# The order of 2,836 steps: an SSM convolution beside linear attention, on one core

## The chip, the core and the metric

The kernel runs on one core of a Trainium2 chip. The core has a tensor engine (PE), a vector engine (DVE), a scalar engine (ACT), GpSimd (POOL) and a queue that issues DMAs (SP). The metric is the time of one execution on the device, in microseconds (us); lower is better.

## What is computed

Two halves are computed and joined along the last axis. The first is a state-space convolution over 2,048 positions and 576 channels, the second an attention with a learned feature map over 32 heads of 18.

```python
# A: K from 128 complex exponentials per channel, then a long convolution by FFT
P = jnp.exp((A * dt[:, None])[:, :, None] * pos[None, None, :])
K = 2.0 * jnp.einsum("dn,dnl->dl", C, P).real
y = jnp.fft.irfft(Uf * Kf[None, :, :], L2)[:, :, :L]      # Uf, Kf: rfft of u and K
a = y + u * D_skip
# B: two softmaxes per head as features, linear attention, an output projection
pq = jnp.einsum("bhsd,hdf->bhsf", q, w_phi)               # pk likewise
phi_q = jnp.concatenate([_softmax(pq, axis=-1), _softmax(-pq, axis=-1)], axis=-1)
kv = jnp.einsum("bhsf,bhsd->bhfd", phi_k, v)
o = jnp.einsum("bhqf,bhfd->bhqd", phi_q, kv) / den
b = o @ wo
return jnp.concatenate([a, b], axis=-1)
```

## The kernel before

All of the work is written first as a list of 2,836 operations, and only then issued. `Plan.op` (line 195) records one operation: its engine, what it reads and writes, and a function that issues its instructions. `body` (line 428) makes the list. `Plan.run` (line 229) goes through the text `ORDER` (line 279 on), takes the operations in that order, gives each buffer the slot that `ORDER` names, and issues them. Each engine works through its own instructions strictly in that order and waits with semaphores for the others.

An entry of `ORDER` reads as follows: the number of the operation; `*` when the second of two possible engines takes it; `!` when ACT loads a function table ahead of it; `+28` for 28 warm-up matmuls; and, after slashes, the slots of the buffers that it is the first to use. Many copies out of PSUM can go to ACT or DVE (`copy`, line 450, whose instructions stand under L453), many elementwise steps between SBUF tiles to DVE or POOL (`tt`, line 460, under L463). There are eight PSUM banks (`ps`), and nearly every PE step needs one to four of them.

The stages, in the names of the code:

- `fold` (497): `wphi` is folded into the key and query weights, in five pieces of heads. Each piece loads a block of the weight (tiles `e`, `ub`, `kvb`) and multiplies it with `wphi` (tile `fT`). PE's output goes into `wh` and `wl`, the high and low parts of the weight. `whole` (524) splits the other weights the same way.
- `key_tile` and `query_tile` (621, 686): 16 tiles of 128 positions each. A projection of 14 matmuls per half or third (`gemm`, 557), two softmaxes (`softmax`, 579: maxima and minima L586 and L587, exponential on ACT L594, pair sums on POOL L597, sums on DVE L598), and products over the heads. The query tiles turn their features by PE transposes (L701), multiply them with the key-value block `kvb`, and project the result.
- `u_first`, `group`, `k_first`, `product`, `last` (757, 926, 975, 1024, 1110): the convolution, by short Fourier steps on PE and elementwise products on DVE. `group` makes the exponentials: PE spreads magnitudes into three banks (L939's loop), ACT takes exponentials (L946), DVE multiplies them with sines and cosines (L950, L467, L954, L956) into `cs` and `E`, and PE sums them in 32 short matmuls, which the profile shows as 64.

Every matrix product is issued from line 448, every DVE or ACT copy from 453.

Of the kernel before, what the change touches and what calls it, by code (L numbers as in the profile page):

```python
# [284 lines left out]
1504 387 1332 1290/5/3/1/7/6 55/4 1293 1333 1292 43/7 1503 275/1 1508 1501 1465 1330/8 388*/2 1291 1328 1466 56/5 274
1502 48 1331/9 1507 1467 1339/1 276/10 131/3 59/0 1509/8 1340 44 389* 1334 1335 45 1510 1336 272/6 234/9 390 73 58 61
391/10 1337 60/9 1197/4 185/11 1294 132/7 62 277 392/2 278 212/12 1468 239/13 240/5 393/3 241* 213/11 63 394 1256/0
1341 214* 1237/14 280*/2 1469 381/3 398 1338 64*/4 215* 65* 1343 57/7 1505/1 104/15 1238/12 74 1344 1519 396 399*
1207/16 270/0 66! 1345 1208/10 242* 273/5 1342 290 369/17 1512 1346 1470 133* 1239 217/7 221/4 134 1199/14 1347/18 395
67/3 289 220 222/3 1426/1 1472 1672 1473 243/1 1511 1471 1531/0 1387/1 279 245/5 250/3 262*/13 1513 1514 1427 281 282  # L290
251 246/3 68/1 252/8 1385 1428 1348 69/0 218/6 263 1386 1198 70* 1533 1200/5/7/4/1/12 1515 1516 71* 75* 76 283/4 1201*
1202* 1506 223 1517 1388 261 284/0 1474/3/0/5/13/9 1476 1255 1429 1518 1520 1204 1477 1430 224 226/1 244/7 1481 1480
1203 1475 247 248 158/8 1431 159/2 1296 347/3 348/5 235 1674 1295 1479 135/2 378/3 216/4 138/4 155/4 1534 225 349*
1487/6/5/1/6/0 1488 249 1679 285/4 227 1490 1521/6 160* 350* 207/14 1522 153 400 1432 1209 286* 1489 228 1523 54/5
219/4 253*/0 254 236 255 1524 1478 1495 287 1492 1482 137/7 1491 428/18 154 429/1 1493 1494 1525 256/16 1206 257/0
1526 229/6 1350 136/4 140/3 1240/1/6/0/3/11 230/1 1527 1241 1496/5/7/4 1528 430* 1483/1 1244 231/2 1433 1529 1217/1
1242 1484 1219*/6 1530 232 1243 1257/3 1205 139 1535/0 143 141/9 142 145/1 455/12 258/5 1536 1434 1485 237* 144 353/3
370 1166 1177/16 161 352/0 1486 1245 146* 355/1 233 356 1497 1437/1/7/4/13/12 431 1537 1498 359 351/6 358 1435 1436
1246 357/0 360 1440! 1499 354/6 1439 1444 1450/5/3/0/6/5 361/2 1538 1442 238 371 362 1453 1456 1218* 1455 1539 1540
1451 1443 1452 1458 1454 147 1438 435/6 434/4 148/1 401/8 402/3 452/9 363 1541 1441 1457 291 439/2 1210/1/5/6/0/11  # L300
1459/3 1213 1445 1212 440 1446/7 451* 441/5 1675 1211 1460 1680 259 432/7 1220/1/4/5/6/6 149/0 364/10 1317/18 1681/1
450 1214 1223 1676 1215 164/0 264 1224 365/4 1544 1221 150/1 1532 366/3 433/6 260 1683 367* 1682 372* 368* 1259/10
1685 403* 1545 1258 163/1 404* 1684 151* 156 456/12 1187/6 1216 169/3 1389/1 1390 1222 1226 152 186/1 437 1447 1225
1461 1448 436 1449 1542 170 1543 167 265 1462 438 442/0 373 1686 1687 166 408/3 168/0 181/13 443 171 1391 457*
1546/0/1/6/6/8 1547! 425* 1392 1548 1559/7/4/5/11/13 1393 1561 1351 1560 1550 1567 1563 1566 1562 172/0 157 173 77/8
1565 406/3 1549 1394 1352 1353 180 405/8 407/0 105/9 1554 410/0 444 445/4 165/4 1552 1551 1564 174 458 461/5 175/17
1395 1553 1396 413 446/3 447/2 106 1673 1677/0 182 412 424 187* 107* 1688 1689 188* 293/3 448* 1555/4 99/4 414/3
1568/1 1397 1400/0/6/7/6/8 1846 1556 1557 1403 1558 409 1401 467/3 411 466 1402 449 176/1 1690 1407 177/4 1405 459/9
1569 294/11 1570 1572/0 1406 415/5 192/4 1404 1573 1574 416 460/3 463 1408 417 209 162/10 190/7 464 1575 1576 292 178
1398 418/17 419/1 1399 194/5 179 1409/6 1571 478/11 453 1678 468/10 193 1577 420/2 189/11 465 1691 320/15 421*  # L310
1413/5/1/0/2/13 1307/12 1415! 1416 1692 469*/1 1178/7 1705/1 1693/17 1578 109/4 470* 1694 477 426* 1695 1696 471 1410
472/17 191/3 1414 1697 195/6 1844 1421 1417 321/8 322* 1411 1579 462/7 479 473/1 196 1698 1277/1 323 1699 1581 1419
422 1700 111/5 1580 1851 324/12 427 1418 1420 1422/1 128 474/2 112/3 1583/5/0/7/3/12 113 1585! 183 197 1412 1423* 198
108/13 1586 325/6 1701 208 1424 1425 475 480 1702 114/2 1584 1591 1781/1 110/3 476 1588 1587 1782 1582 1783
1622/5/4/1/13/1 1590 1624! 1589 199/2 329/5 1703 115 328 1784 116 117 1592/7 1593 1227/15 1625 200 330/3 326/0 1623
1785 327/6 1630 1786 201 78/12 118/2 1847 1626 1852 496/17 1628 127 1787 1629 202/0 344 1627 119 120 1594 184 203/3
1596 295* 1179 1631/1/8/9 1632 1854 1598/6/4/3/5/0 296* 297/14 343 1744/0 1595 1790 1863 1602 1853/3 1597 1601 1856
79* 332 1633 299/7 80 1634 1745 331 1788 1599 333 204/2 1600 1604/3/5/0/1/1 1606 1789 121/8 1267/16 1855 122/1 123/4
454 304/0 1791 298/5 484 1608 1746 1747 1748 305 334*/6 1318*/9 306/5 1607* 205* 1605* 316*/8 301 302 303 1704 335
1706 1792/7/1/3/7/13 1794! 1799 1800 1319* 1793 1795 1798 1797 336 300/0 317 307/6 1260/1/5/4/6/11 1264 481 124 1261  # L320
1749 1262 1796 1603/1 483 1805/6/3/0/0/10 1806 1263* 1807 83/1 1808 337/18 308 309 100 82/4 338/1 1609 1813 1750
1269*/11 1751 339/6 210 206 1812 89/0 81/15 1188*/18 504/1 1753 88 1811 211 1810 1809 90/6 1801/0 1610/1/6/3/7/7 125
1266 1857 340* 1802 1612 84/5 129* 1754 1752 341 86 85 91*/4 1611* 511/13 310/3 506/1 1279*/14 87 92 1803 1804 1858
1614* 1613 311/0 1265 312/1 313* 315 1297/10 1859 130 93 1616/3/7/0/4/12 1619 1814/6 101* 1617* 1848 1620*
1320/3/5/4/0/0 318 1618 1322* 1323* 1615 94/5 509 1324 505/7 1815* 1321 1860 507 1635/1 510 1180/4/3/5/0/10 1184 1183
# [831 lines left out]
```

## Time and profile before

| what | value |
|---|---|
| median of three runs | 514.7 us (512.82 to 516.24) |
| the profiled execution's own time | 511.89 us |
| its span, first to last instruction | 510.1 us |
| PE, matmuls busy | 485.1 us, 95% |
| PE, weight loads busy | 406.6 us, 80% |
| DVE busy | 450.0 us, 88% |
| ACT busy | 400.6 us, 79% |
| POOL busy | 337.0 us, 66% |
| DMA, 16 engines | 71.3% by the main queue, mean 226 GB/s |
| mean granted TensorE clock | 0.993 |

The profile is one execution. A row of its timeline has a start and a duration in us, the engine, the line, the instruction and what it writes and reads; a number in brackets at the end is the time that the engine stood idle before, and what released it. "issue" there means that nothing the profile shows was waited for. A row of the groups ends with busy time, mean nanoseconds of one instruction, and idle time before them. Busy time of PE counts matmuls with modelled ends.

### The profile page before, as it was taken

What the parts mean: (1) busy time and instruction counts of PE and PEld (TensorE: products, weight loads), DVE (VectorE), ACT (ScalarE), POOL (GpSimd) and SP (SyncE); (2) the same over time, 40 slices, a digit from 0 to 9 for tenths busy, and PEclk for the clock granted to TensorE, in tenths of its full rate; (3) what the DMA queues carried; (4) which work ended last, traced back from release to release, by engine and by line L of the source; (5) the groups of instructions that cost most, each with busy time, mean ns of one, the idle gap of its engine ahead of it and who ended that gap; (6) DMA issues with size and microseconds to landing.
All of it is one profiled execution on the core that took longest, in us unless ns stands there. A gap on an engine that the chain in (4) does not pass through costs nothing.

```text
span 510.1 us, 20535 instructions
## 1 busy us (share of the span) xinstructions
PE 485.1 (95%) x8544; PEld 406.6 (80%) x8544; DVE 450.0 (88%) x999; ACT 400.6 (79%) x704; POOL 337.0 (66%) x405
## 2 busy tenths in 40 slices
PE   5999999999999989899999999998999999999997
PEld 5999798899988878688886767775788886677976
DVE  3899999999999998999898999998999688889584
ACT  5589889899999989999999888999897535545321
POOL 1653599679878897996895379887465326476510
PEclk9799999999999999999999999999999999999999
DMA  7976974615507476771999386649696998998797
GB/s 204 351 255 189 306 219 171 190 39 197 186 27 234 143 231 192 196 255 34 302 272 352 100 267 212 215 142 298 202 324 176 330 272 245 294 370 254 269 324 213
DMA packets 80800, 115.45 MB, mean 226 GB/s; under 512 B 12612, under 2 KB 58564, under 8 KB 80708
## 3 DMA queue, kind: packets, MB, share of 16 engines
q1 hardware_dynamic: 80708, 114.14, 71.3%
q8 instruction: 67, 1.10, 0.9%
q14 instruction: 25, 0.20, 0.1%
HBM read 65.11 MB, written 49.01 MB: 224 GB/s over the span
## 4 chain that ended last, share of the span: by engine, by line
PE 57%; DVE 17%; ACT 15%; issue 4%; DMA 4%; SPq 1%; POOL 1%; DVEq 0%; ACTq 0%
PE ps L448 53%; PE ps L701 3%; ACT ps L946 2%; ACT cs L914 2%; ACT cs L922 2%; DMA e<-in_wkT_dram 2%; ACT cs L921 2%; DVE cs L950 1%; DMA x<-xd 1%; ACT e L594 1%; DVE x L463 1%; PE ps L731 1%; DVE small L463 1%; ACT zi L453 1%; DVE e L467 1%
## 5 line engine op out<-in xcount | busy, mean ns | idle before, releaser
L448 PE MATMUL ps<-wh,x 128*128 128x288 f32 (+2 forms) x1008 | 242.5, 321 | 2.2 <-DVE ks L467 1.0
L448 PEld LDWEIGHTS ps<-wh,x 128*128 128x128 f32 x1008 | 173.7, 189 | 14.8 <-issue 3.7
L448 PE MATMUL ps<-wl,x 128*128 128x288 f32 (+2 forms) x560 | 175.3, 314 | 0.9 <-issue 0.9
L448 PEld LDWEIGHTS ps<-wl,x 128*128 128x128 f32 x560 | 105.7, 189 | 1.3 <-issue 1.2
L904 POOL TENSOR_TENSOR cs<-cs,pi 128x64 int32<-128x64 int32 (+4 forms) x90 | 90.1, 1001 | 5.0
L463 POOL TENSOR_TENSOR E<-v,cs 128x512 f32<-128x512 f32 x34 | 43.2, 1287 | 25.7 <-ACT v L946 25.7
L597 POOL TENSOR_TENSOR o<-e 128x576 f32<-128x576 f32 x32 | 43.2, 1351 | 21.5 <-ACT e L594 12.7
L946 ACT ACTIVATE ps<-ps 128x512 f32<-128x512 f32 x90 | 50.0, 589 | 6.4 <-PE ps L448 5.9
L467 DVE TENSOR_TENSOR ac<-us,ps 128x576 f32<-128x576 f32 x64 | 44.7, 745 | 6.0 <-PE ps L448 5.8
L950 DVE TENSOR_TENSOR cs<-ps,cs 128x1024 f32<-128x1024 f32 x36 | 43.6, 1216 | 2.7 <-ACT ps L946 2.5
L594 ACT ACTIVATE e<-e 128x1152 f32<-128x1152 f32 x32 | 37.3, 1171 | 9.1 <-POOL e L463 9.0
L448 PEld LDWEIGHTS ps<-E,cs 128*32 128x32 f32 x2304 | 34.0, 110 | 8.8 <-issue 3.5
L448 PE MATMUL ps<-E,cs 128*32 128x64 f32 x2304 | 39.0, 220 | 1.7 <-DVE E L956 1.3
L922 ACT ACTIVATE cs<-cs,hp 128x1024 f32<-128x1024 f32 x36 | 40.3, 1146 | 0.0
L463 POOL TENSOR_TENSOR e<-e,small 128x576 f32<-128x576 f32 x26 | 32.2, 1239 | 11.7 <-DVE small L463 11.0
L453 ACT ACTIVATE zi<-ps 128x288 f32<-128x288 f32 x91 | 33.1, 410 | 8.6 <-PE ps L448 6.6
L921 ACT ACTIVATE cs<-cs 128x1024 f32<-128x1024 int32 x36 | 37.5, 1057 | 0.2
L463 POOL TENSOR_TENSOR e<-small,e 128x576 f32<-128x576 f32 x26 | 30.4, 1170 | 10.1 <-DVE small L463 2.4
L463 POOL TENSOR_TENSOR ac<-ac 128x288 f32<-128x288 f32 x31 | 24.3, 810 | 16.0 <-DVE ac L467 14.2
L914 ACT ACTIVATE cs<-cs 128x2048 f32<-128x2048 int32 x18 | 34.6, 1924 | 0.1
L886 POOL TENSOR_TENSOR pi<-pi 128x192 int32<-128x192 int32 (+1 forms) x42 | 21.1, 513 | 17.5 <-DVE pi L882 10.1
L586 DVE TENSOR_REDUCE small<-ps 128x16 f32<-128x288 f32 (+2 forms) x64 | 28.3, 444 | 4.9 <-PE ps L448 4.8
(144 smaller groups left out, 1005.3 us busy)
## 6 DMA issues: line engine op xcount, KB each, us to landing
dram<-zi SPq DMA_DIRECT2D x32, 288.0 KB
xd<-x SPq DMA_DIRECT2D x16, 576.0 KB
dram<-zi SPq DMA_DIRECT2D x16, 576.0 KB
x<-xd SPq DMA_DIRECT2D x16, 576.0 KB
kb<-dram SPq DMA_DIRECT2D x32, 288.0 KB
ub<-dram SPq DMA_DIRECT2D x32, 288.0 KB
dram<-zo SPq DMA_DIRECT2D x32, 288.0 KB
zi<-dram SPq DMA_DIRECT2D x16, 576.0 KB
```

What stands on the lines that cost most here:

```text
L448: pe.matmul(o, l, r, start=start, stop=stop, skip_group_check=skip)
L453: op(("act", "dve"), (c_act(n), c_dve(n)), lambda e: act.activation(dst(), src(), AF.Copy) if e == "act" else dve.tensor_copy(dst(), src() ...
L463: op(eng, [c_dve(n[0]) if e == "dve" else c_pool(n[1]) for e in eng], lambda e: (dve if e == "dve" else pool).tensor_tensor(dst(), a(), b( ...
L467: op(eng, c_dve(n) if eng == "dve" else c_pool(n), lambda: e.tensor_tensor(dst(), a(), b(), op=alu), r=r, w=w, with_=with_, lock=eng == "p ...
L594: op("act", c_act(1152) + 40, lambda: act.activation(e.t, e.t, AF.Exp), r=[e], w=[e], table="exp")
L597: op("pool", c_pool(517), lambda: pool.tensor_tensor(pair.t, e.t[:, :, :, 0:9], e.t[:, :, :, 9:18], op=ALU.add), r=[e], w=[pair], lock=True)
L904: op("pool", c_add(4 * n * W), lambda n=n, j=j: pool.tensor_tensor(x()[:, :, :, n:2 * n], x()[:, :, :, 0:n], pi.t[:, j:j + 2, gs].bitcast( ...
L914: op(("act", "dve"), (c_act(n) + 45, c_dve(n)), lambda e: act.activation(cs.t[:, 0], x(), AF.Abs) if e == "act" else dve.scalar_tensor_ten ...
L921: op("act", c_act(64 * W) + 150, lambda at=at: act.activation(at(1), at(1).bitcast(I32), AF.Sin, scale=TURN), r=[cs], w=[sine], with_=[cs] ...
L922: op("act", c_act(64 * W) + 225, lambda at=at: act.activation(at(0), at(0), AF.Sin, scale=-TURN, bias=hp.t), r=[cs, hp, sine], w=[both], w ...
L946: op("act", c_act(512) + 12, lambda x=x, y=y: act.activation(y.t, x.t, AF.Exp), r=[x], w=[y], table="exp")
L950: op("dve", c_dve(64 * W), lambda: dve.tensor_tensor(F(), both(M.t), F(), op=ALU.mult), r=[M, ready], w=[long], with_=[cs])
```

## The change

Only the text `ORDER` is replaced. The operations, their dependences, the numbers of slots and all functions stay as they are. The new text was found by a search that began at the old one, with a model of the chip corrected for late results, late instructions and extra waits.

```diff
 ORDER = """
-0/0 3 2 1 423/0 33 1356 1357 1362 4/1 35+28/0 34/1 49/2 1361 1363/2 1364 1366 1365 1367 1368 482 1373 5/0 342/2 1369
+0/0 1 2 234/0 1349 4/1 288/2 1354 1358 1357 1362 1356 1361 1363/3 5/0 7+28/0 1364 1365 1366 1367 1368 1369 1370 6/1
...
```

PE takes its 414 steps in nearly the same order as before: a step moves by less than one place on average and by nine at most. DVE's, ACT's, POOL's and SP's steps move by five to eleven places on average, and almost all slots are other ones, PSUM banks included. 74 copies out of PSUM go from ACT to DVE and 55 the other way; 27 elementwise steps go from DVE to POOL and 19 the other way. So DVE has 1,010 steps rather than 999, ACT 627 rather than 646, POOL 409 rather than 401. ACT loads its function tables 43 times in both. PE's stream holds 196 separate wait instructions rather than 189, ACT's 200 rather than 193, DVE's 207 rather than 219.

Three places, as the instructions stand.

The first is SP's queue at the very start. `e`, `ub` and `kvb` are the five blocks of the key weight, `fT` is `wphi`, `zo` a tile of x; `cre`, `cim`, `dt`, `th` are small parameters of the convolution. Before:

```order
L504 DMA kvb<-in_wkT_dram 72x640
L841 DMA cre<-in_cre_dram 128x96
L841 DMA cim<-in_cim_dram 128x96
L500 DMA fT<-in_wphi_dram 128x630
L504 DMA e<-in_wkT_dram 126x640
L839 DMA dt<-in_ldt_dram 128x96
L841 DMA th<-in_aim_dram 128x96
L504 DMA ub<-in_wkT_dram 126x640
L491 DMA zo<-in_xT_dram 128x640
L504 DMA e<-in_wkT_dram 126x640 x2
```

In the changed kernel the same queue begins so:

```order
L500 DMA fT<-in_wphi_dram 128x630
L839 DMA dt<-in_ldt_dram 128x96
L841 DMA cim<-in_cim_dram 128x96
L841 DMA cre<-in_cre_dram 128x96
L504 DMA e<-in_wkT_dram 126x640
L841 DMA th<-in_aim_dram 128x96
L504 DMA ub<-in_wkT_dram 126x640
L504 DMA e<-in_wkT_dram 126x640
L491 DMA zo<-in_xT_dram 128x640
L504 DMA kvb<-in_wkT_dram 72x640
L504 DMA e<-in_wkT_dram 126x640
```

The block in `kvb` moves from the front to the tenth place, the x tile behind the second `e`; the last `e` is the eleventh load in both. PE's fold follows: before, `kvb`, `e`, `ub`, `e`, `e`; now `e`, `ub`, `e`, with `kvb` between the pieces of that `e`, and the last `e`.

The second is DVE at the sixth pair of groups, just before the short matmuls that start at 212 us in the profile of before. `E<-ps,cs` are the products that those matmuls read, `small<-o` is the softmax sum of a query tile. Before:

```order
L467 TENSOR_TENSOR e<-ps,small 128x16x18
L950 TENSOR_TENSOR cs<-ps,cs 128x2x16x32
L467 TENSOR_TENSOR E<-ps,cs 128x16x32 x2
L954 TENSOR_TENSOR E<-ps,cs 128x16x32
L598 TENSOR_REDUCE small<-o 128x64
L956 SCALAR_TENSOR_TENSOR E<-ps,cs 128x16x32
L600 RECIPROCAL small<-small 128x32
```

In the changed kernel, at the same place of DVE's stream:

```order
L467 TENSOR_TENSOR E<-ps,cs 128x16x32
L950 TENSOR_TENSOR cs<-ps,cs 128x2x16x32
L467 TENSOR_TENSOR E<-ps,cs 128x16x32
L954 TENSOR_TENSOR E<-ps,cs 128x16x32
L956 SCALAR_TENSOR_TENSOR E<-ps,cs 128x16x32
L598 TENSOR_REDUCE small<-o 128x64
L600 RECIPROCAL small<-small 128x32
```

The softmax sum moves behind the last product, and one of the E products ahead of the cs product.

The third is PE at another group, at 377 us in the profile of before. `ps<-E,cs` are the group's 32 short matmuls, `ps<-kvb,fT` end a query tile's products, `wh` and `wl` with a numbered x begin or end a projection, and `ident,o` are transposes of a query tile. Before:

```order
L448 MATMUL ps<-kvb,fT 64x95 x2
L448 MATMUL ps<-kvb,fT 64x76 x2
L448 MATMUL ps<-E,cs 32x64 x32
L448 MATMUL ps<-wh,x_6823 128x288
L448 MATMUL ps<-wl,x_6823 128x288
```

In the changed kernel:

```order
L448 MATMUL ps<-wh,x_6636 128x288 x2
L448 MATMUL ps<-wl,x_6636 128x288
L448 MATMUL ps<-E,cs 32x64 x32
L731 MATMUL ps<-ident,o 128x128 x4
L732 MATMUL ps<-ident,o 128x128
```

The projection of 14 matmuls that followed the group now stands ahead of it.

More of the change, by code (lines that the diff above doesn't have):

```diff
@@ L285 @@
[L285 to L324, printed above, removed]
@@ new lines @@
+1285 1035/1 1836* 1833* 1286 2162 1036/0 1834 1037/0 1889 1032/5 1033/2 1838/6/3/2/7/0 1034 1189* 1038/5/1 857 1835
+1887 1840* 1933* 1936/0/4/11 706/0 1839* 707 1039/9 1841* 1837 1842* 1940/2/6/3/5/3 1040 1937* 858/2 855/7 1943!/0
+1041 1938 2019 2020 1942 1843 1042 1228* 1941 1939 708 1947 1944 1230/0/1/3/4/6 1233 1232 1234 859 860 1946* 1948
+1945* 1231 1236 861 1043/5 1045/0 2164 709/3 2166 710/2 1310/0/4/1/2/0 1312 1313 862/3 863 1949/6 1953/1
+1890/4/5/7/8/12 1314* 711 1311 712 1235 1954 1950 1316 1190/0/2/1/3/3 1951 1952 713* 1891 1892 1044/6 1893/6 1192
@@ new lines @@
+2327 2333 2725/5/1/13 2726 2727 670/0 2760/4/7/17 2761 1062 2728 2762 1063* 2623/1/6/3/2/1/15 671/0 1064 672 2763
+765/7/0 2737 766/3 767 673 2758 2730 2627* 2729 674* 2624 777/5 2764 782/0 972/4 976/3 781 2628/0 783/4 2629/5 2625
+977 679/2/2 680 971/7 973 2765 776/5 974 979*/5 2603/8 2602/16 978/10 677/4/13 2626 975 768 778 779 769 784/3 2522/10
+675/7/17 2630/3/2/6/1/2/13 780 678 2631 676 2767/0/4/0 2768 681/7 2635 2632 2773/11 814/12 785 786 2769
+2597/4/6/3/5/5/17 2601 2599 787/1 980 2598 2636 2637 2638 2633 2634 2770 2757 2521/7 682/0 2600 684/2 685/1
@@ new lines @@
+2604/1/5/0/6/8/0 2680/15 683/2 686 2681/13 2675/4/7/3/2/11/8 2678 2772 2513/16 2606 2610 1065/5/18 2771 2676* 2576/4
+788/1 1066 1067/6/12 2609 687/4/3 688/7 2605 2607 689 1068 2677 2608 2679* 690 770/5 772/5 2515/1 691
+2639/4/7/6/1/17/2 2640 2682/2/0/5/3/5/1 1069/4/9 789 2611 2612 2642* 692/6 1070 2641* 2569/0 2643* 2683 2684 2685 2688
+2687 2644/1 2570/13 2613/0/2/1/4/11/15 2616* 2614* 1071/7 2645 1074/5 2707/6 981 2615 694*/18 1075/0 1072/2
+2516/0/1/2/3/8/9 2518 790 791 2519 2618 1073/17 1076 794/6/12 2617* 2568/1 792/5/14 795 2523/4/1/7/2/0/8 2689 2517*
@@ L425 @@
+2827 2749 2750 1105 847 2781/7/3/13 2782* 1008 1113/2 2809/4/6/17 2810* 1114/3 813 2751 2811 2812 1115/16 2816/1/5/1
+2813 2830/6/3/7 2831* 2832 2833 2835 2817 2834 2783 2784 1110/5 1111/3 2786 2814 2785 2828 1112 2795/3/2/5 2788/6/4/11
+2789 2802/7/0/8 2790 2791 2796 2793 2803* 2818 2819 2804 2820 1116/4/5 2792 849/2 1117/2 1118 1119 2805 1120 2806
+848/1 2797 2821 2798 2800 2807 851*/13 2799 850 852 1122/5 1124/6 1121/1 1123* 1125
 """.split()
```

229 lines of the change are left out of this document (125 added, 104 removed).

## Prediction

> **What bounds the kernel now.** I read the page first (busy times, the chain that ended last), then the busy time of every engine in stretches of 50 us, because shares over the whole span mix the stages.
>
> ```profile
> span 510.1 us, 20535 instructions
> PE 485.1 (95%) x8544; PEld 406.6 (80%) x8544; DVE 450.0 (88%) x999; ACT 400.6 (79%) x704; POOL 337.0 (66%) x405
> PE 57%; DVE 17%; ACT 15%; issue 4%; DMA 4%; SPq 1%; POOL 1%; DVEq 0%; ACTq 0%
> ...
> 50.00:100.00 50.00, 47.68 (x860) 42.90 (x859) 48.73 (x106) 43.48 (x75) 38.01 (x49) 1.00 0.70 217
> 100.00:150.00 50.00, 50.00 (x801) 47.37 (x803) 47.88 (x102) 46.89 (x69) 42.38 (x52) 1.00 0.35 121
> 150.00:200.00 50.00, 47.14 (x1142) 39.31 (x1128) 46.80 (x106) 46.88 (x81) 43.10 (x46) 1.00 0.66 209
> 200.00:250.00 50.00, 47.02 (x758) 40.53 (x759) 47.32 (x115) 48.76 (x83) 41.50 (x53) 1.00 0.59 173
> 250.00:300.00 50.00, 47.45 (x1021) 37.17 (x1009) 46.08 (x104) 44.41 (x87) 32.60 (x35) 1.00 0.80 248
> 300.00:350.00 50.00, 47.73 (x1123) 35.70 (x1106) 46.33 (x102) 47.23 (x78) 43.29 (x50) 1.00 0.70 219
> 350.00:400.00 50.00, 47.72 (x988) 38.84 (x992) 45.36 (x101) 40.51 (x62) 27.95 (x26) 1.00 0.78 249
> 400.00:450.00 50.00, 49.46 (x869) 37.73 (x861) 39.91 (x90) 24.83 (x60) 21.72 (x27) 1.00 0.94 285
> ```
>
> The columns are PE, PE's weight loads, DVE, ACT and POOL, then TensorE's granted clock and the DMA engines. The tensor engine is busy 95% and carries 57% of the chain, so it bounds the kernel. But up to 350 us DVE and ACT are busy 44 to 49 of every 50 us as well: they give the banks free and make the operands that PE waits for. From 400 us on only PE is full. PE stands idle 510.1 - 485.1 = 25.0 us. Of these 15.8 us lie between 50 and 450 us (400 less the sum of the eight PE numbers, 384.2). The rest is mostly the start and the last store. An order that runs the same matrix work can win from these 25 us, and from waits hidden in PE's busy time, since matmul ends are modelled; little else.
>
> **The change, part by part.** The operations and PE's work are the same, and PE's own order moves by a few places. What changes is the start, who stands before whom on DVE and ACT, the banks, and which of two engines takes a copy or an elementwise step.
>
> *The start.* These rows give the sizes of the first loads, PE's first real work, and the clock.
>
> ```profile
> e<-in_wkT_dram SPq DMA_DIRECT2D x3, 315.0 KB
> fT<-in_wphi_dram SPq DMA_DIRECT2D x2, 315.0 KB
> ub<-in_wkT_dram SPq DMA_DIRECT2D x1, 315.0 KB
> kvb<-in_wkT_dram SPq DMA_DIRECT2D x1, 180.0 KB
> zo<-in_xT_dram SPq DMA_DIRECT2D x16, 320.0 KB
> cre<-in_cre_dram SPq DMA_DIRECT2D x6, 48.0 KB
> ...
> 6.55 1.32 PE L448 MATMUL ps<-fT,e 126*128 126x126 f32 x10
> 9.79 1.38 PE L448 MATMUL ps<-fT,ub 126*128 126x126 f32 x10 [1.92 <-DMA ub<-in_wkT_dram]
> 12.67 4.63 PE L448 MATMUL ps<-fT,e 126*128 126x126 f32 x20 [1.50 <-DMA e<-in_wkT_dram]
> 16.96 0.66 PE L448 MATMUL ps<-wh,x 128*128 128x378 f32 x1
> ...
> 8.00:9.00 1.00, 0.00 (x0) 0.00 (x0) 0.26 (x1) 0.98 (x2) 0.00 (x0) 1.00 0.93 291
> 11.00:12.00 1.00, 0.17 (x2) 0.00 (x0) 0.57 (x2) 0.63 (x1) 0.00 (x0) 0.78 1.04 224
> 16.00:18.00 2.00, 2.00 (x10) 2.00 (x9) 1.05 (x3) 1.09 (x3) 0.61 (x1) 0.50 1.11 398
> ```
>
> PE waits twice for a load of wkT, 1.92 and 1.50 us. Before the `ub` load stand 180 + 315 + 315 KB and four loads of 48 KB; with itself 1317 KB, and PE starts at 9.79. Before the second `e` come 320 KB more; with itself 1952 KB, and PE starts at 12.67. So the queue delivers (1952 - 1317) / (12.67 - 9.79) = 220 KB/us. In the new order the 180 KB load stands behind both and the 320 KB load behind the second: `ub` is in after 1137 KB, 0.8 us earlier (9.0), the second `e` after 1452 KB, 2.3 us earlier (10.4). The last `e` closes the same 2267 KB in both, at 12.67 + 315/220 = 14.1. Ten matmuls take 1.32 us at full clock, so the fold may end at 15.4, at half clock at 16.7; before, the first projection starts at 16.96. That is a gain of 0.3 to 1.6 us; I take 1.0. Other ends: if the 180 KB load, now ahead of the last fold pieces, comes a microsecond late, 1.0 is lost; if the clock did not fall at all, the 5.7 us of PE work between 12.67 and 18.4 would shrink by half of that, 2.9 more.
>
> The clock rows show 1.00 until PE has idled at 8 us and 0.50 at 16 to 18. [...]
>
> *Results that come late.* The second place is the waves' group whose matmuls start at 212.18.
>
> ```profile
> 212.18 1.10 PE L448 MATMUL ps<-E,cs 128*32 128x64 f32 x64 [1.30 <-DVE E L956]
> ...
> 210.15 0.68 DVE L954 TENSOR_TENSOR E<-ps,cs 128x512 f32<-128x512 f32 x1
> 210.77 0.75 DVE L598 TENSOR_REDUCE small<-o 128x64 f32<-128x576 f32 x1
> 211.44 0.68 DVE L956 SCALAR_TENSOR_TENSOR E<-ps,cs 128x512 f32<-128x512 f32 x1
> ```
>
> PE waits 1.30 us for the last E. On DVE a softmax sum (L598) stands ahead of it. In the new order it stands behind: E starts at 210.77 instead of 211.44, and 0.67 us of the 1.30 are gone. What is late next is the softmax sum, some 0.6 us later than before; PE's next step but one needs it, behind a POOL step. Of the 15.8 us of idle time, 5.7 are of another kind (below), so 10.1 are waits for results. This place gives half of its wait back. Other places get more lead, and others less, so the ends are 5.2 worse (the added DVE work, below) and 5.0 better (half everywhere). I take a quarter, 2.5 us, as nearer to the gain because the work on PE's path was moved forward where I looked and nothing there was moved back.
>
> *Code that comes late.* Some idle rows name no releaser. I found six; the first, the longest and the last:
>
> ```profile
> q8 instruction: 67, 1.10, 0.9%
> 186.99 0.44 PE L448 MATMUL ps<-e,v 128*19 128x36 f32 x27 [0.98 <-issue]
> 350.67 0.77 PE L701 MATMUL ps<-ident,e 128*128 128x128 f32 x5 [2.12 <-issue]
> 378.43 0.53 PE L448 MATMUL ps<-E,cs 128*32 128x64 f32 x19 [0.32 <-issue]
> ```
>
> PE's 2 x 8544 instructions come in 67 pieces, about 255 each. All six idle rows start at the same place of such a piece, counted through PE's stream, and the first and the longest follow many short matmuls. So PE ran out of code. The six last 0.32 to 2.12, in all 5.7 us. Short matmuls placed together use a piece up fastest. At 378 the new order puts a projection of 14 long matmuls ahead of the group's short ones: that row goes, 0.3 us. At 350 only the transposes trade places, and around 187 the stretch stays as dense. I take -0.3; the ends are 2.4 better (350 goes too) and 2.1 worse (one more like it).
>
> *Work that changes engine.* On DVE there are 22 more copies out of PSUM and 3 fewer of the `fT` kind, and from DVE to POOL go, net, seven splits of x and five small sums, while three `kb` steps and one of 576 columns come back.
>
> ```profile
> L453 DVE COPY zi<-ps 128x288 f32<-128x288 f32 x37 | 15.8, 447 | 3.5 <-PE ps L448 3.5
> L453 DVE COPY fT<-ps 128x512 f32<-128x512 f32 (+1 forms) x15 | 7.4, 498 | 5.6 <-PE ps L701 5.6
> L463 DVE TENSOR_TENSOR x<-zo,x 128x512 fp32r<-128x512 f32 (+1 forms) x24 | 13.3, 553 | 1.0 <-ACT x L543 0.8
> L463 DVE TENSOR_TENSOR small<-small 128x32 f32<-128x32 f32 x22 | 7.5, 343 | 0.3
> L463 DVE TENSOR_TENSOR kb<-ub 128x288 f32<-128x288 f32 x12 | 7.3, 607 | 0.0
> L463 DVE TENSOR_TENSOR e<-e,small 128x576 f32<-128x576 f32 x6 | 4.9, 819 | 0.0
> L453 ACT ACTIVATE zi<-ps 128x288 f32<-128x288 f32 x91 | 33.1, 410 | 8.6 <-PE ps L448 6.6
> ```
>
> The copies: 22 x 0.447 - 3 x 0.498 = 8.3 us more on DVE. The rest: 7 x 0.553 + 5 x 0.343 - 3 x 0.607 - 0.819 = 2.9 less. Net 5.4 us more, about 5.2 as one of the copies is only of 128 columns. ACT is relieved of 19 x 0.410 = 7.8 us. DVE has 60.1 us idle (510.1 - 450.0), which hides it: I put 0 into the sum, and the 5.2 into the rival below.
>
> DVE's `kb` step with two operands in SBUF takes 607 ns, the copy of the same size out of PSUM 447. [...]
>
> **Sum.** 511.9 (the profiled execution, its span and 1.8 us around it) - 1.0 - 2.5 - 0.3 = 508.1. The median shown, 514.7, is 2.8 above the profiled execution, so the median of the changed kernel comes to **510.9 us**, 0.7% below. Its own range is 506.5 to 515.
>
> **Rivals.** *The waits go further (faster).* Half of the result waits go (5.0), the start takes 1.6, the code waits at 350 and 378 both go (2.4): 511.9 - 9.0 + 2.8 = 505.7, with 501 as its end. For it: waits of this kind cost PE more than its idle rows show. Against it: PE's order hardly moves, and where 44 to 49 of 50 us are used on three engines, each step moved ahead puts another back.
>
> *DVE becomes the late engine (slower).* Between 150 and 350 us DVE is busy 186.5 of 200 us. Between 150 and 400 us 14 copies more, net, come to DVE, and each gives a bank free that a later matmul writes, while the steps that left for POOL were on nobody's path. If each copy holds PE up for its 0.447 us, that is 6.3 us; with nothing won elsewhere, 511.9 + 6.3 + 2.8 = 521.0. It decides from 12 of the 14 on (5.2 us, 1% of 514.7). Against it: the same copies leave ACT, which is as full.
>
> *The trades cancel* (no gain, 512 to 517): the order shows that steps did move, but PE's floor is the same; this lies within my forecast's case.
>
> **How the numbers follow.** Within 1% is about what a measurement of this kernel can tell from no change (its three runs spread over 512.8 to 516.2). Forecast and cancelling trades together, within 1%: 0.44. Further gain, faster by over 1% (below 509.6): 0.40. DVE late, slower (above 519.8): 0.16. The range 501 to 520 leaves out the best end of the first rival (0.05) and most of the second (0.15).
>
> **What would show it.** PE's fold row with `ub` at about 9.0 and the second `e` at about 10.4, the first projection before 16.7. The E row of that group without L598 ahead of it and PE's wait there about 0.6. No issue row inside the group's matmuls that now follow the projection near 378, but one still near 187. DVE busy about 455, ACT about 392, PE's idle time 21 rather than 25. Wrong would be: PE's waits for DVE between 150 and 400 us grown by microseconds, or new issue rows of over a microsecond.

## The result, and the profile after

The changed kernel takes 510.75 us, median of 22 runs (507.23 to 514.91), against 515.15 for the kernel before in the same job (22 runs, 509.91 to 519.78). The ratio is 0.9919 with a 95% interval of 0.9897 to 0.994: 0.8% faster, 4.2 us. The profiled execution took 507.23 us, against 511.89. Here and below a ratio leaves out executions more than 1.5% above the fastest one of their kernel, a median does not, and the profiled executions of the runs with two places, shift and copies were such long ones.

These are the span, the busy times and the chain of waits on the page of the changed kernel, and below them three stretches of the table by windows, with its sum over 50 to 450 us.

```profile
span 505.4 us, 20522 instructions
PE 482.6 (95%) x8544; PEld 404.6 (80%) x8544; DVE 454.6 (90%) x1010; ACT 394.9 (78%) x684; POOL 340.0 (67%) x413
PE 69%; DVE 15%; issue 4%; DMA 4%; POOL 3%; ACT 2%; SPq 1%; DVEq 0%; POOLq 0%; ACTq 0%
```

```profile
50.00:100.00 50.00, 49.16 (x827) 44.54 (x813) 48.97 (x102) 42.65 (x74) 40.08 (x55) 1.00 0.68 211
100.00:150.00 50.00, 50.00 (x897) 47.35 (x896) 49.40 (x103) 49.01 (x69) 43.59 (x54) 1.00 0.30 106
...
400.00:450.00 50.00, 48.20 (x855) 35.81 (x857) 43.33 (x97) 19.91 (x49) 26.18 (x33) 1.00 0.94 287
sum 400.00, PE 386.13 PEld 321.24 DVE 373.73 ACT 335.52 POOL 300.28; mean PE 48.27 PEld 40.15 DVE 46.72 ACT 41.94 POOL 37.53
```

PE now carries 69% of the chain instead of 57%. It stands idle 505.4 - 482.6 = 22.8 us (before 25.0), and 400 - 386.13 = 13.9 us of it lie between 50 and 450 us (before 15.8). Between 50 and 150 us, where it stood idle for 2.3 us, it stands idle for 0.8. Between 400 and 450 us it stood idle for 0.5, and now for 1.8: something was gained early, and something lost late.

The start, in PE's timeline of the changed kernel, and the clock in two windows there:

```profile
6.45 1.35 PE L448 MATMUL ps<-fT,e 126*128 126x126 f32 x10 [1.90 <-DMA e<-in_wkT_dram]
8.19 2.50 PE L448 MATMUL ps<-fT,ub 126*128 126x126 f32 x10 [0.38 <-DMA ub<-in_wkT_dram]
10.48 1.34 PE L448 MATMUL ps<-fT,e 126*128 126x126 f32 x8
...
13.12 1.41 PE L448 MATMUL ps<-fT,e 126*128 126x126 f32 x10
14.35 0.44 PE L448 MATMUL ps<-wh,x 128*128 128x378 f32 x1
```

```profile
8.00:10.00 2.00, 1.81 (x8) 1.81 (x9) 1.08 (x6) 1.33 (x6) 0.00 (x0) 0.50 0.99 269
...
14.00:16.00 2.00, 2.00 (x14) 1.99 (x13) 2.00 (x7) 1.65 (x3) 1.84 (x4) 1.00 1.03 385
```

`ub` is there at 8.19 (forecast 9.0), the second `e` by 10.48 (forecast 10.4), and the last `e` makes nothing wait at 13.12, so it was in before the 14.1 that the prediction gave it. The clock is at 0.50 in the window from 8 us and at 1.00 from 14 to 16, where it was at 0.50 before. The first projection begins at 14.35, 2.6 us earlier.

The second place, the short matmuls of the sixth pair of groups, in the timeline of the changed kernel:

```profile
204.40 0.68 DVE L956 SCALAR_TENSOR_TENSOR E<-ps,cs 128x512 f32<-128x512 f32 x1
...
205.00 0.74 DVE L598 TENSOR_REDUCE small<-o 128x64 f32<-128x576 f32 x1
...
205.20 1.10 PE L448 MATMUL ps<-E,cs 128*32 128x64 f32 x64
...
207.76 1.20 PE L701 MATMUL ps<-ident,e 128*128 128x128 f32 x9 [1.46 <-POOL e L463]
```

L956 now has the softmax sum (L598) behind it, and the wait of 1.30 at the short matmuls is gone. The next step on PE, the transposes of `e`, waits 1.46 us for POOL. In the kernel before the row of these transposes reads:

```profile
214.10 1.20 PE L701 MATMUL ps<-ident,e 128*128 128x128 f32 x9 [0.83 <-POOL e L463]
```

So 0.63 us of the 1.30 are back one step later.

These are all idle rows of PE in the changed kernel, from 16 us on, that name no releaser:

```profile
189.19 0.78 PE L448 MATMUL ps<-fT,e 72*128 72x72 f32 x5 [1.88 <-issue]
268.00 0.35 PE L448 MATMUL ps<-kvb,fT 128*64 128x76 f32 x3 [0.23 <-issue]
336.79 1.10 PE L448 MATMUL ps<-E,cs 128*32 128x64 f32 x63 [0.40 <-issue]
352.98 0.38 PE L448 MATMUL ps<-sel,mg 32*128 32x256 f32 x2 [0.74 <-issue]
364.58 0.74 PE L448 MATMUL ps<-ac,ff 32*32 32x288 f32 x21 [0.21 <-issue]
419.37 0.69 PE L448 MATMUL ps<-ub,ff 64*32 64x288 f32 x7 [0.81 <-issue]
458.98 0.67 PE L448 MATMUL ps<-ac,ff 32*32 32x288 f32 x3 [1.45 <-issue]
```

They add up to 5.72 us, against 5.67 of the six before. Counted through PE's stream of matmuls, weight loads and waits, all six of before stand 194 places behind a multiple of 256, and these seven 193 or 194. The row inside the group near 378 is gone, the one near 187 has grown from 0.98 to 1.88, and behind 400 us there are two where there was none.

What went away are waits for DVE in the first 170 us. The rows of the kernel before, and then those of the changed kernel in the same part of the work:

```profile
52.34 0.75 PE L448 MATMUL ps<-kb,w 32*64 32x288 f32 x16 [0.29 <-DVE small L463]
53.88 0.75 PE L448 MATMUL ps<-e,v 128*19 128x36 f32 x64 [0.80 <-DVE v L463]
...
99.64 0.45 PE L448 MATMUL ps<-wh,x 128*128 128x396 f32 x1 [1.01 <-DVE ks L467]
...
160.22 0.57 PE L448 MATMUL ps<-sel,mg 32*128 32x256 f32 x6 [0.44 <-DVE v L453]
```

```profile
51.06 0.57 PE L448 MATMUL ps<-sel,mg 32*128 32x256 f32 x5 [0.51 <-DMA mg<-gd]
...
85.19 0.86 PE L448 MATMUL ps<-kb,w 32*64 32x288 f32 x16 [0.26 <-DVE e L467]
```

2.54 us of waits became 0.77.

### The profile page after: what moved, and what is told of

It reads as the page before. It is cut to its first block, busy times and chain, and to the rows that moved or that the text cites. A ratio compares the mean times of both kernels' runs of the same rounds, so it can differ in the third digit from the quotient of the medians.

```text
span 505.4 us, 20522 instructions
## 1 busy us (share of the span) xinstructions
PE 482.6 (95%) x8544; PEld 404.6 (80%) x8544; DVE 454.6 (90%) x1010; ACT 394.9 (78%) x684; POOL 340.0 (67%) x413
## 4 chain that ended last, share of the span: by engine, by line
PE 69%; DVE 15%; issue 4%; DMA 4%; POOL 3%; ACT 2%; SPq 1%; DVEq 0%; POOLq 0%; ACTq 0%
PE ps L448 65%; PE ps L701 3%; DVE cs L950 2%; DVE E L467 2%; POOL cs L904 2%; PE ps L731 1%; DVE E L956 1%; DMA kb<-dram 1%; DMA gd<-cs 1%; DVE x L463 1%; DVE E L954 1%; DVE ac L467 1%; DMA ub<-in_wkT_dram 1%; DMA mg<-gd 1%; DVE e L467 1%
## 5 line engine op out<-in xcount | busy, mean ns | idle before, releaser
L463 POOL TENSOR_TENSOR e<-small,e 128x576 f32<-128x576 f32 x24 | 28.2, 1174 | 10.7 <-DVE e L467 9.8
L453 ACT ACTIVATE zi<-ps 128x288 f32<-128x288 f32 x80 | 28.9, 413 | 5.3 <-PE ps L448 5.0
```

The lines of the kernel that those rows point to most:

```text
L453: op(("act", "dve"), (c_act(n), c_dve(n)), lambda e: act.activation(dst(), src(), AF.Copy) if e == "act" else dve.tensor_copy(dst(), src() ...
L463: op(eng, [c_dve(n[0]) if e == "dve" else c_pool(n[1]) for e in eng], lambda e: (dve if e == "dve" else pool).tensor_tensor(dst(), a(), b( ...
```

## The experiments

The theory after this comparison was that the start gives the larger part of the gain, since PE is 2.6 us ahead there of 4.2 in all, that the engine choices cost nothing, and that late code gives nothing. The rivals: the start is worth the 1.0 us of the prediction and the rest lies in later waits; the copies on DVE cost time that something else wins back; the gain lies in where the pieces of code happen to begin. Every run is compared with the kernel before on the same chip, with 10 or 12 executions of each (6 where it is far slower) against 27 to 29. The kernel before had medians of 513.4 to 514.2 us in these jobs.

### The loads and the fold of the new start alone

In the text of the order this is the beginning:

```diff
-0/0 3 2 1 423/0 33 1356 1357 1362 4/1 35+28/0 34/1 49/2 1361 1363/2
+0/0 3 2 1 423/0 4/1 1354 1357 1362 1356 49/2 1361 1363/2
...
+5/0 7+28/1 6/0 126/5 1369 1355 1358 1370 19/4 21/3 1359/0 1360
```

> The kernel before, with only the start of the changed kernel: the order of the first eleven loads, of the ten fold steps on PE with their banks, of the copies and low parts that empty them, and the one clearing of a tile on POOL that has to wait for the old place of the 180 KB block. Everything from the first projection on is as before. If the start is the larger part of the gain, the first projection begins at 14.3 to 15.0 us rather than 16.96, its first matmuls run at full clock, and the time falls by 2.6 to 3.3 us (ratio 0.9935 to 0.995). If the start is worth the 1.0 us of the prediction, because what PE wins there it waits for again in the first projections (for x tiles and copies), the ratio is 0.997 to 0.999. If the whole gain came from later waits, the ratio is 1.000.

Measured: 515.61 us, ratio 1.0044 (1.0011 to 1.0078): slower, which none of the three expected. PE's timeline:

```profile
14.20 1.98 PE L448 MATMUL ps<-fT,kvb 72*128 72x72 f32 x8 [2.36 <-DVE wl L516]
...
18.91 0.66 PE L448 MATMUL ps<-wh,x 128*128 128x378 f32 x1
```

In the new order of the fold a bank comes round sooner. The low part that has to empty it stood on DVE behind the split of an x tile, PE waited 2.36 us, and the first projection began at 18.91, 2 us later than before. The loads are no gain without the steps on DVE and POOL that go with them.

### The whole start

As above, and DVE's, ACT's and POOL's order up to the first projection too, with the x split (376, 377) on POOL and one `kb` step (1249) on DVE.

```diff
-19/4 21/5 126/5 374/6 12/1 375/0 376* 1377 377*
+374/6 33 10 1377 1378 1379 26/2 375/0 376 1380 377 8 49/2 22 11
```

> The kernel before with the whole start of the changed kernel: loads, fold and banks as in the run with the new start, and also the order of DVE, ACT and POOL up to the first projection, with the first x split on POOL instead of DVE and one kb step on DVE instead of POOL. Behind the first projection everything is as before. In the run with the new start alone PE waited 2.36 us in the fold for a low part (wl, L516) on DVE, which stood behind the x split. If that wait was all that spoiled it, the first projection begins at 14.3 to 14.8 us and PE stays 2.6 to 3.3 us ahead to the end, since the 2 to 3 us that the earlier run had lost by 30 us were still lost at the end: ratio 0.993 to 0.996. If later steps take the lead back (loads of x and u, which this order does not move), PE is ahead by less than 1 us at 60 us and the ratio is 0.998 to 1.002.

Measured: 512.45 us, ratio 0.9987 (0.9963 to 1.0012): 0.7 us, with an interval from 1.9 better to 0.6 worse. In its timeline the first projection comes at 15.07. Then come three rows around the sixth pair of groups, and the window with the clock behind the second:

```profile
15.07 0.44 PE L448 MATMUL ps<-wh,x 128*128 128x378 f32 x1
...
209.86 1.10 PE L448 MATMUL ps<-E,cs 128*32 128x64 f32 x64 [1.30 <-DVE E L956]
211.78 2.01 PE L701 MATMUL ps<-ident,e 128*128 128x128 f32 x9 [0.82 <-POOL e L463]
...
220.23 1.58 PE L448 MATMUL ps<-kvb,fT 128*64 128x76 f32 x40 [0.37 <-ACT fT L453]
```

```profile
211.00:214.00 3.00, 2.22 (x17) 1.89 (x25) 3.00 (x6) 2.47 (x6) 3.00 (x3) 0.67 0.78 213
```

Up to 209.86 PE is 2.3 us ahead of the row at 212.18 of the kernel before. At 220.23 it is 1.2 ahead of the same row there, which reads:

```profile
221.41 1.63 PE L448 MATMUL ps<-kvb,fT 128*64 128x76 f32 x40 [0.37 <-ACT fT L453]
```

Between the two the clock fell to 0.67, right behind waits of 1.30 and 0.82 us that lie together; in the profile of before two such waits (1.30 and 0.83) left it at 1.00 over the whole stretch from 200 to 250 us. So the lead of 2.3 us was carried through 190 us of work, and 1.1 of it went in the stretch with this one fall of the clock. For the other executions no trace shows where their part went.

### The changed kernel with the old start

```diff
-0/0 2 1 234/0 1349 4/1 288/2 1354 1358 1357 1362 1356 1361 1363/3 5/0 7+28/0
+0/0 2 1 234/0 49/4 33 288/2 1356 1357 1362 1361 4/1 1363/3 5/0 35+28/2
```

> The changed kernel with the start of the kernel before put back: loads, fold, the order of ACT and DVE up to the first projection, the x split on DVE and the kb step on POOL. The rest is as changed. If the start is worth 3.3 us of the 4.4, this lies at a ratio of 0.997 to 1.000 to the kernel before and the first projection begins at about 17. If the start is worth 1.0, as predicted, the ratio is 0.993 to 0.995, and the gain lies in what follows.

Measured: 510.96 us, ratio 0.9943 (0.9916 to 0.9971). Against the 0.9919 of the changed kernel, measured in another job, the start is worth 0.0024, 1.2 us, with 1.8 either way (the half intervals added as squares), and what follows it 0.0057, 2.9 us, with 1.4 either way. The run before gave 0.7 for the start and allows 1.9 at most, so the theory falls. The prediction's 1.0, about a quarter of the gain, fits both runs, but neither of them tells it from nothing.

The 2.6 us at the first projection are one pair of executions, too. In the six profiles with the old loads and no filler it begins at 15.90 to 18.65 us, 17.3 in the mean, and in the five with the whole new start and no filler at 14.35 to 15.68, 15.1 in the mean.

### The clock held up by filler

```diff
-35+28/0
+35+37/0
-21/5
+21+17/5
-13/7
+13+13/7
```

> The kernel before with more idle matmuls on zeros at the start: 37 rather than 28 ahead of the first fold piece, 17 in the wait for the ub load, 13 in the wait for the second e load. Nothing else moves. If the clock is what the start loses, it stays at 1.00: the twenty matmuls that took 4.63 us from 12.67 on take 2.6 to 2.8, the first projection begins at 15.2 to 15.5 and its first 1.4 us run at full clock too, in all 2.0 to 2.9 us less (ratio 0.994 to 0.996). If the loads are the limit, the last e makes PE wait until 14.1 and the gain is about 0.7 to 1.5. If the clock falls for another reason than idle PE, nothing changes. The 39 matmuls more are also 78 more instructions in front of everything else in PE's stream. If the idle rows without a releaser (186.99, 196.11, 274.85, 281.47, 350.67, 378.43) are late pieces of code, they do not stay at their work: each turns up about 78 instructions earlier in the work, longer or shorter as the work there uses code up faster or slower, and the 2.12 us in front of the transposes near 350 are gone from there. If they are waits for something that the profile does not show, they stay where they are.

Measured: 516.03 us, ratio 1.0038 (1.0005 to 1.007): slower. The wait for `ub` and the end of the fold:

```profile
10.57 1.38 PE L448 MATMUL ps<-fT,ub 126*128 126x126 f32 x10 [0.84 <-DMA ub<-in_wkT_dram]
...
13.22 2.91 PE L448 MATMUL ps<-fT,e 126*128 126x126 f32 x20
```

The twenty matmuls took 2.91 us instead of 4.63, with the clock at 1.00 (the window below). But `ub` came 0.8 us later in this execution (10.57 for 9.79), then a copy (ACT, 0.58) became the limit, and the first projection came at 16.71, only 0.25 us earlier. At the wait for `v` PE was 0.9 us ahead (52.97 for 53.88), and it stayed about so up to 190 us.

All six rows without a releaser of the kernel before are gone from their work, the one ahead of the transposes near 350 too, and seven others stand elsewhere. In PE's stream they stand as before: all seven 193 or 194 places behind a multiple of 256, and four of them (near the 6,082nd, 8,642nd, 8,898th and 11,970th place) where four of the six stood. The wait keeps to its place in the stream while other work comes to stand there. That fits pieces of code (the page of the kernel before and that of the changed kernel show 67 packets of the instruction queue, about 255 of PE's matmuls and weight loads each) and not a hidden wait of the work itself.

In the end the kernel is 0.4% slower. In these two profiles the rows without a releaser do not account for it (5.96 us for 5.67). From 16 us on, PE's waits for DVE grew from 6.2 to 8.5 us and those for ACT from 1.8 to 2.9; why is open. The window of the clock:

```profile
12.00:17.00 5.00, 4.42 (x35) 3.76 (x33) 4.36 (x13) 4.25 (x12) 3.00 (x8) 1.00 1.03 347
```

### Code moved by 34 places in the changed kernel

```diff
-7+28/0
+7+45/0
```

> The changed kernel with 45 rather than 28 idle matmuls on zeros ahead of the first fold piece, where PE waits 1.9 us for a load anyway. It moves every later instruction of PE by 34 places in its stream and costs PE nothing at the start. If late code depends on where the pieces of about 256 instructions begin in the work, and the order was fitted to that, the idle rows without a releaser all move to other work and grow together, and the time is 3 to 8 us longer: ratio to the kernel before 0.998 to 1.008. If the pieces do not matter, the time stays within 1 us of the changed kernel's 510.7, ratio 0.990 to 0.994, perhaps a little less because the clock does not fall at 7.7 us.

Measured: 515.12 us, ratio 1.0 (0.9962 to 1.0039). 17 idle matmuls, put where PE waits anyway, cost 4.2 us (2.3 either way), as much as the whole gain. The first projection begins at 15.56, as in the other profiles with this start. The longest of its ten rows without a releaser:

```profile
351.41 0.83 PE L701 MATMUL ps<-ident,e 128*128 128x128 f32 x3 [3.23 <-issue]
```

The rows have moved to other work again, and one of 1.01 us, at 56 us, is in a stretch where neither kernel had any. In this profile the ten add up to 12.44 us, against 5.72; that the other executions lose as much there is not shown. So the gain of the changed kernel also hangs on the places at which its code breaks into pieces. For the order before this is not shown: under the filler its rows add up to hardly more (5.96 for 5.67).

### Two of the moves alone

```diff
-1139/6 630 1654
+630 1654 1139/6
-2254/6 ... 738/3
+738/6 ... 2254/3
```

> The kernel before with two of the moves of the changed kernel alone: on DVE the softmax sum (L598) behind the last E product ahead of the short matmuls at 212.18, and on PE the projection of 14 matmuls ahead of the group's short matmuls near 377 (with their two banks exchanged). The first: E starts at 210.8 rather than 211.44 and PE's wait of 1.30 there falls to about 0.6. If that is a gain, PE stays 0.6 us ahead at 220; if it is given back, the wait for POOL at the next transposes grows by about as much (0.9 to 1.5). The second: the idle row without a releaser inside the short matmuls (0.32) goes. Together 0.3 to 0.9 us if neither is given back (ratio 0.998 to 0.9995), 0 to 0.3 if the first is.

Measured: 513.89 us, ratio 0.9981 (0.9945 to 1.0018): no difference that can be seen. At the first place:

```profile
215.65 1.10 PE L448 MATMUL ps<-E,cs 128*32 128x64 f32 x64 [0.60 <-DVE E L956]
...
218.27 0.99 PE L701 MATMUL ps<-ident,e 128*128 128x128 f32 x7 [1.52 <-ACT wh L531]
```

The wait is 0.60 instead of 1.30, exactly as worked out, and the next wait 1.52 instead of 0.83. From the E row to the transposes the kernel before takes 214.10 - 212.18 = 1.92 us, this one 218.27 - 215.65 = 2.62. All 0.70 us are given back, and the order of the two DVE steps explains it. The transposes wait for POOL's step on `e`, that step for the reciprocal (L600), and the reciprocal stands on DVE behind the last product and the softmax sum in either order. In the kernel before:

```profile
212.04 0.34 DVE L600 RECIPROCAL small<-small 128x32 f32<-128x32 f32 x1
```

In this one:

```profile
216.29 0.35 DVE L600 RECIPROCAL small<-small 128x32 f32<-128x32 f32 x1
...
217.05 1.16 POOL L463 TENSOR_TENSOR e<-e,small 128x576 f32<-128x576 f32 x1
```

From the start of L954 to the reciprocal it is 1.89 us before (210.15 to 212.04) and 1.97 here (214.32 to 216.29), and to the transposes 3.95 in both. The profile names ACT's L531, which ended 0.07 us behind POOL's step. At the second place the row without a releaser inside the group is gone, as expected.

### Only the engine choices, in the old order

175 entries gain or lose their `*`; two of them:

```diff
-1254 ... 1201* 1202*
+1254* ... 1201 1202
```

> The kernel before in its own order and banks, with only the choice of engine taken from the changed kernel: 74 copies from ACT to DVE, 55 the other way, 27 elementwise steps from DVE to POOL, 19 the other way. By the prediction the 5 us more of DVE work are hidden: DVE busy about 455, ACT about 393, the ratio 0.998 to 1.003. By the rival in which DVE becomes late, each copy more holds PE up: PE's waits for DVE grow between 150 and 350 us and the time is 5 to 6 us longer, ratio 1.010 to 1.013. A third way: the choices only fit the order they were searched with, and in the old order steps of both directions wait, ratio over 1.005 with waits for ACT and POOL as well as DVE.

Measured: 543.42 us, ratio 1.0581 (1.0532 to 1.0631). PE's waits in sum:

```profile
PE ps L448 <- DVE e L467: 4.3, 5, 2.3
PE ps L448 <- DVE zi L453: 3.3, 5, 1.3
PE ps L731 <- ACT zo L453: 2.2, 1, 2.2
```

The columns are sum, times and the longest in us. It is the third way in that copies on both engines are waited for, DVE's (`zi`) and ACT's (`zo`), and a DVE step (`e`) besides. Idle time is not all of it. Between this profile and that of the kernel before, spans of 543.2 and 510.1 us, PE's idle time grew from 25.0 to 40.4 us, and the mean granted clock fell from 0.993 to 0.975, an estimated 10 us (0.025 of 543.2 less 0.007 of 510.1).

### Only the copies, in the old order

As above without the 46 elementwise steps between DVE and POOL.

> The kernel before with only the copies' engines of the changed kernel: 74 from ACT to DVE, 55 the other way; the elementwise steps between DVE and POOL stay. All engine choices together cost 30 us in the old order. If the copies that now stand in DVE's queue among other work are what holds PE up, this run costs most of the 30 us (ratio 1.04 to 1.06) with PE's waits named by DVE copies and by what stands behind them. If it is the steps moved to POOL, this run lies near the kernel before (ratio under 1.01), and the rest of the 30 us belongs to POOL.

Measured: 542.97 us, ratio 1.0557 (1.051 to 1.0603). The copies alone cost 5.6 of the 5.8%, and the intervals show no part of the steps on POOL.

### The old copies in the new order

> The changed kernel with the old engines of its copies: 74 go back from DVE to ACT and 55 from ACT to DVE; the order of everything stays as changed. Putting the new engines into the old order cost 28 us. If engines and order are one choice, this costs much too, ratio 1.03 to 1.06 to the kernel before, with PE's waits named by copies. If only more copies on DVE hurt, because DVE is then the late engine, this one has 19 fewer there and lies at 0.99 to 1.00.

The edit is the reverse of the last one, on the changed kernel. Measured: 539.08 us, ratio 1.0477 (1.0419 to 1.0534), 5.6% slower than the changed kernel. PE's largest wait in sum:

```profile
PE ps L448 <- ACT us L453: 5.0, 2, 3.5
```

This kernel has 19 copies fewer on DVE than the changed one and waits most for copies on ACT. So it is not that DVE has too much: either set of engines costs about 29 us in the order of the other.

### The two orders joined at 270 us

The entries of one order up to 270 us of its own profile, and what is left in the order of the other. At the seam of the first of the two:

```diff
 2025/0 2026 2027 1900* 724/1 725/17 722
-872/0/11 939 1901 726/1/5 2028 1913 2029 1914
+892/13 2162 2166 2169 1913 1901 726/2/0 727/5
```

> The order, engines and slots of the kernel before up to 270 us (the first 1,551 of 2,836 entries), and from there the order and engines of the changed kernel, its slots renamed so that buffers alive at the seam stay where they are. With the start worth 1.0 us and the rest of the gain 2.9 us, the question is where the rest lies. If it is spread evenly over 20 to 500 us, this kernel wins 1.4 us: ratio 0.996 to 0.999. If it lies in the first half, the ratio is 0.999 to 1.003. If it lies in the second half, 0.993 to 0.996. Instructions that the seam puts late can cost up to 1 us once, seen as a wait near 270.

Measured for the old order and then the new: 516.94 us, ratio 1.0061 (1.0029 to 1.0093). It decides little, because the seam itself is in it:

```profile
278.02 2.17 PE L448 MATMUL ps<-ub,ff 64*32 64x288 f32 x32 [4.39 <-ACT fT L453]
```

That wait exists in neither kernel and is about as long as the whole effect looked for.

> The other way about: the changed kernel's order up to its 270 us, the old one from there. Evenly spread: 1.0 and 1.5, ratio 0.994 to 0.997. All of the rest in the first half: 0.991 to 0.994. All in the second half: 0.997 to 1.000. If the two halves add up, this gain and that of the other seam come to 4 us together; if they do not, the gain hangs on how the halves fit, for example on where the pieces of code begin.

Measured for the new order and then the old: 507.68 us, ratio 0.9893 (0.9858 to 0.9928), the lowest of all runs. Its rows without a releaser:

```profile
188.11 0.78 PE L448 MATMUL ps<-fT,e 72*128 72x72 f32 x5 [0.94 <-issue]
267.95 0.35 PE L448 MATMUL ps<-kvb,fT 128*64 128x76 f32 x3 [1.26 <-issue]
342.67 0.39 PE L448 MATMUL ps<-sel,mg 32*128 32x256 f32 x2 [1.19 <-issue]
```

With one of 0.16 at 179 us they add up to 3.55 us, and there is none behind 343 us: the rows at 419 and 459 belong to the new second half (old start has them at 425 and 465, old then new at 430 and 469). The seam costs a wait here too, which neither kernel has at this place:

```profile
272.25 0.40 PE L448 MATMUL ps<-wh,x 128*128 128x288 f32 x1 [1.18 <-DVE ac L467]
```

This kernel is 0.26% faster than the changed one, but the two intervals overlap, so it is at least as fast and not surely faster.

### The same seam at 220 us

> The changed kernel's order up to its 220 us, the old one from there. With the seam at 270 it tells whether the stretch from 220 to 270 matters. Evenly spread: ratio 0.995 to 0.997. If the stretch up to 220, with the group at 205 and the late code near 190, holds the rest of the gain, 0.991 to 0.994; if it holds none of it, 0.997 to 0.999, the start alone.

Measured: 510.82 us, ratio 0.9952 (0.9922 to 0.9981), 2.5 us. Between this run and the last are 0.0059, 3.0 us, with an uncertainty of about 2.4 (the two half intervals of 0.0035 and 0.003 added as squares). That is not what the new order wins between 220 and 270 us, because the seam is in it, and in the profile also a late piece of code ahead of the seam:

```profile
189.56 1.00 PE L448 MATMUL ps<-fT,e 72*128 72x72 f32 x5 [2.46 <-issue]
...
223.66 0.52 PE L731 MATMUL ps<-ident,o 128*128 128x128 f32 x3 [1.51 <-DVE E L956]
```

The second wait exists in neither kernel. The first stands in code that this run shares with the last and with the changed kernel, and there it is 0.94 and 1.88 us.

The profiles tell more than this difference. Take in each the moments at which PE has done the matrix work that the kernel before has done at 20, 170, 220 and 270 us (an estimate: each matmul counts with the usual time from its start to the next in the kernel before). From 20 to 170 us the changed kernel gains 2.7 us on the kernel before, old start 3.8, and the two joined with the new order first 3.4 and 4.3. Shift gains 0.7, with 2.5 us of rows without a releaser in that stretch. The kernels with the old order there gain 0.1 or less (new start, whole start, filler, two places, old then new). From 220 to 270 us the new order loses 0.6 to 0.7 us in each of four profiles (changed kernel, old start, shift, new then old). So what the new order wins behind the start, late code aside, it wins in the main before 170 us.

The four waits for DVE shown above at 52.34, 53.88, 99.64 and 160.22, 2.54 us together, lie in this stretch. The two of 0.80 and about 1.0 us come back in the profiles of the kernels with the old order there (new start 0.80 and 0.99, whole start 0.80 and 1.10, old then new 0.80 and 0.99), and in none with the new order there (old start, shift, both joined with the new order first). Which of the moves took them away, no run isolates.

## Why the prediction came out as it did

The forecast was 510.9 and the median is 510.75. That the two agree to 0.15 us is luck: the profiled execution came 0.9 us below the 508.1 of the sum, and the median lies 0.7 us further above it than was added. The largest term has the right size. But two of the terms are right for other reasons than the prediction gave.

**What bounds it.** Right. PE's chain share rose to 69%. Of the 4.7 us between the two spans 2.2 are idle time of PE (22.8 for 25.0; 21 was forecast), and 2.5 are its busy time, of which the clock explains an estimated 2 (0.007 of 510.1 less 0.003 of 505.4, by mean granted clocks of 0.993 and 0.997).

**The start, 1.0 us.** To the end it is worth 0.7 or 1.2, by the two runs, which fits and does not prove it. Its working was too low, though: the first projection came 2.6 us earlier in this pair of profiles and 2.2 in the mean of all, not 0.3 to 1.6. The step that failed is the last load, put at 14.1 by one rate of the queue. PE took it at 13.12 without a wait, so the queue had delivered (2267 - 1137) / (13.12 - 8.19) = 229 KB/us or more, and in the kernel before the arrival of that load could not be seen, since nothing waited for it. The clock fell at another time, too: it is at 0.50 from 8 to 10 us, at 0.73 from 10 to 12 and at 1.00 from 12 on, through the first projection, where it was at 0.50 from 12 to 18 us before. What moved the fall forward is not shown. With the same start, whole start and new then old took 2.48 and 2.47 us for their first ten matmuls (1.35 in the changed kernel), though the granted clock of new then old is 1.00 in the mean from 0 to 20 us (0.91 in the changed kernel); why is open. And with the old loads, the run with the engine choices alone took 0.41 us for the first matmul of its first projection (0.44 in the changed kernel, 0.66 before). Of the 2.6 us over half is lost again before the end. One profile shows 1.1 of it go where the clock fell to 0.67, at 211 us; for the rest the place stays open.

**Late results, 2.5 us.** The size holds (2.9 us behind the start, 1.4 either way), the evidence for it didn't. The group at 212 us, the place that the prediction worked out, gives nothing: the swap alone takes 0.70 from one wait and adds 0.70 to the next. The wrong steps there were "gives half of its wait back" and "what is late next is the softmax sum". Nothing comes later: the transposes hang on the reciprocal, which stands behind both DVE steps in either order, and so nothing could be won. The gain arises before 170 us, where four waits for DVE went that the prediction did not look at. PE's waits for DVE between 150 and 400 us, named as a sign of being wrong if they grew by microseconds, fell from 4.1 to 2.0. The second half of the new order wins nothing and loses perhaps 1.3 us (0.9919 against 0.9893, with intervals that overlap).

**Late code, 0.3 us.** The reading as late pieces of code held: the rows keep their places in PE's stream, 193 to 195 behind a multiple of 256, when the work is moved by 78 or 34 places. The row at 378 went as forecast. The sum was not right: 5.67 us became 5.72. Around 187, where "the stretch stays as dense" and no change was put in, 0.98 became 1.88, and new rows of 0.81 and 1.45 came at 419 and 459. "New issue rows of over a microsecond" was named as a sign of being wrong, and one came. The length of a single row is no firm number, though: at one place of the same code the profiles show 0.94, 1.88 and 2.46 us (near 189), and 0.23 and 1.26 (at 268). The ends of 2.4 and 2.1 were too narrow as well: the same order with its code 34 places further costs 4.2 us more.

**Work that changes engine, 0 us.** The busy times came as forecast (DVE 454.6 for 455, ACT 394.9 for 392), and the time too. The reason was wrong. "DVE has 60.1 us idle, which hides it" is an argument by the sum, and in the old order, with the same work, the same choices cost 30 us, 29 of them by the copies. They cost nothing that can be seen where they were chosen together with the order. The rival in which DVE becomes late priced this at 0.447 us for each net copy more; what counts is each changed copy, of both directions, and where it stands: 29 us for 129 of them, 0.22 us each on average. The 607 ns of a `kb` step on DVE, 160 more than the copy's 447, are a mean of two kinds. In the kernel before nine of the twelve `kb` steps take 0.39 to 0.45 us, and three take 1.07 to 1.12, each of which ends 0.3 us after a POOL step that it overlaps. What the eight steps more on POOL cost, no run isolates.

**From the profile to the median.** 2.8 us were added for the difference between the profiled execution and the median. After, the difference is 3.5 (510.75 - 507.23).

**The rivals.** "The waits go further" (505.7) did not come, though the new order joined with the old second half reaches 507.7. "DVE becomes late" is what happens when the choices are made without the order.

## What to carry to other kernels

In an order that is nearly full on three engines, price a moved step by what waits next: the wait that goes can come back one step later (0.70 of 0.70 us here). Engine choices and order are one choice (either set of engines cost about 29 us in the other's order); a sum of idle time, here 60.1 us on DVE, does not say that a step can change its engine. A few instructions more at the front of PE's stream can cost as much as a whole search has won (34 places cost 4.2 us here), so compare orders with the places of the code pieces in mind, and try the halves of a new order apart. Where a seam or a single execution may be in the difference, compare the profiles at equal work.

## What the hardware showed that was not expected

The page shows 67 packets of the instruction queue, in both kernels, for PE's 2 x 8544 matmuls and weight loads, about 255 each. Moving the work by 34 places in PE's stream cost 4.2 us of 511 (17 idle matmuls at the front of the changed kernel), with single waits of up to 3.23 us that name no releaser. The rows stand 193 to 195 places behind a multiple of 256 in PE's stream, in both kernels and with filler or shift. In these runs the wait keeps to the instruction count, not to the work, and its length differs from one execution to the next (0.94 to 2.46 us at one place).

The clock fell in the middle of a full stretch: 0.67 between 211 and 214 us, behind two waits of 1.30 and 0.82 us that stand close together. In the profile of before two such waits (1.30 and 0.83 us) left it at 1.00. It also fell behind a single row without a releaser, that of 2.46 us at 189.56 in the run with the seam at 220 us: to 0.66 between 189 and 194 us, which makes 0.97 in the mean of 170 to 220, where new then old has 1.00. Holding the clock at 1.00 through the start made the fold of twenty matmuls 1.7 us shorter (2.91 for 4.63) and the kernel no faster (ratio 1.0038).
